# Segmented attention with a memory, mixed with a gated FFN: two weight loads cut in halves, the gate row spread by its transfer, and the order of the work written anew

## The chip, the cores and the metric

The kernel runs on one core of one Trainium2 chip. The metric is the device time of one execution in microseconds. The kernel before takes 268.12 us, the median of 3 runs (267.37 to 268.38).

In this document TensorE is PE (its weight loads are PEld), VectorE is DVE, ScalarE is ACT, GpSimd is POOL, and SyncE is SP, which here only issues transfers (SPq in the profile).

## The reference

The input x has 2048 rows of 512 numbers, in bf16. Three results are formed from it and mixed row by row:

```python
x = A_x
g = _sigmoid((x * gate_w).sum(-1, keepdims=True))
a = _A_ref(x, A_wq, A_wk, A_wv, A_wo, A_beta)
b = _B_ref(x, B_W_gate, B_W_up, B_W_down)
return g * a + (1 - g) * b
```

`_A_ref` is attention with 32 heads of 16 columns, over 4 segments of 512 rows. Inside a segment it is a causal softmax; in addition each head has a memory matrix M and a norm z, both sums over all earlier segments, and `beta` mixes the two by head:

```python
num = jnp.einsum('bhld,bhde->bhle', pq, M)
den = jnp.einsum('bhld,bhd->bhl', pq, z)[..., None] + 1e-06
o = g * (num / den) + (1.0 - g) * a_dot
```

`_B_ref` is a feed-forward part with 1792 hidden columns, `(relu(x @ W_gate) * (x @ W_up)) @ W_down`.

## The kernel before, in words

**Steps and order.** The kernel doesn't issue its instructions directly. Each piece of work is a step: a name, the engine or engines that may do it, the steps it comes after, and a function that emits it (`Plan.add`). A list of numbers, `ORDER` (lines 41 to 100), then fixes for each engine which step comes when: the number v stands for step v // 5 on engine v % 5 of PE, ACT, DVE, POOL, QSP (the queue of SP). `Plan.lay_out` (line 137) walks these five queues and hands out the PSUM banks; it has costs and landing times of its own, which decide nothing but which of the four banks a step gets. Between engines the tile framework adds the waits that the data need.

**PSUM.** Four banks `rb` of 512 columns take all products but the scores; a step that takes a bank waits until an earlier one has been copied out of it. The scores have one tile, `sp`, of four banks; so a score block waits until the exp of the block before it has read `sp`.

**The step names that matter here.** Digits behind a name are the segment and the index.
- XP, XA: transpose of a tile of x on PE (16 small matmuls for segment 0), and its copy to `xT` (ACT or DVE).
- VI and VC: V of segment 0, one 512-column matmul for each tile t and each quarter ci of the depth (VI30 is tile 3, quarter 0); VC copies it out. All four VI of a tile share a bank. V101 and so on are V products of the next segment.
- Q00, K00 and so on: Q or K of a segment, 128 columns each, four matmuls (line 486); QC, KC copy them out; KO is a masked copy of K; EK and EQ are exps of K and Q for the memory, MN, MQ, PK, PQ what follows them; KX transposes PK's result by a transfer.
- G0_0, U0_0 and so on: 128 hidden columns of W_gate or W_up, four matmuls (line 903); R (relu) and H (product) copy them out.
- QK000 to QK008: nine blocks of scores of a segment's first two units, EX000 and so on their exps (line 755, on ACT, the longest step of ACT), MK the causal mask on POOL, PV the product with V.
- GB and GC: described below. TG: the row sums x * gate_w (line 574, DVE, four of them, one per tile of x); TC, TE follow them.
- YP, YD, YA, YH: the gates by heads, from two small loads into `gin`. YP takes a bank and YD (lines 420 and 421, DVE) frees it.
- XT1: the load of x for segment 1 by a transposing transfer, into the place where segment 0's plain x stood, so it comes after the XP and all TG.
- D, DB, W: the product with W_down in two halves, and with wo, of one tile of rows.

**The start.** x and the weights of segment 0 are loaded by `early` (line 345), outside the ordered queues and in the order of the code: on SP x tile 0, wv's first, third and fourth quarter, x tiles 2 and 3, all of wk, two small gate loads into `gin`, all of wq; on ACT x tile 1, wv's second quarter, and `gate_w` as one row of 1 KB. Behind wq the queue of SP goes on with pieces of W_gate and W_up (columns cut at 256, 768 and 1280).

TG needs `gate_w` on all 128 partitions. The row lands in one partition of a zeroed tile, `grow`; GB multiplies it on PE with a matrix of ones, and GC copies the result to `gwb`:

```python
def row_mm(e, s):
    nc.tensor.matmul(rb[s.bank][:], lhsT=ones[:], rhs=grow, start=True, stop=True)
rm = add("GB", {"PE": 0.3}, row_mm, after=[gr_in], prio=-900.0, take=True, lat=0.25)
```

**Around the change.** Before PE begins on K it waits for the whole of wk; before Q for the whole of wq. The first steps of PE are, in order, the warm-up, XP00 to XP11, VI and GB mixed, XP20, XP21, VI02, VI03, XP31, XP30, then:

```
VI20 VI21 VI22 VI23 VI30 VI31 VI32 K00 K01 Q00 VI33 G0_0 YP QK000 K03 K02 Q03 QK001
G0_1 G0_2 Q01 QK002 U0_1 U0_0 V111 QK003 ...
```

The functions that the change touches:

Of the kernel before, what the change touches and what calls it, by code (L numbers as in the profile page):

```python
# [12 lines left out]
P = 128  # L13
# [28 lines left out]
    69, 125, 130, 140, 160, 136, 150, 167, 350, 156, 355, 146, 375, 215, 380, 221, 385, 390, 170, 180, 397, 360, 176,  # L42
    365, 186, 200, 190, 400, 206, 405, 197, 79, 371, 410, 467, 415, 425, 89, 430, 421, 435, 472, 260, 71, 285, 94,
    267, 250, 272, 292, 84, 440, 1070, 257, 104, 446, 462, 225, 505, 976, 335, 477, 511, 99, 983, 310, 232, 342, 214,
    325, 236, 1081, 242, 518, 996, 520, 1090, 317, 526, 1002, 1110, 1007, 987, 1014, 275, 1101, 533, 332, 1016, 535,
    282, 1095, 994, 541, 322, 1075, 454, 1107, 1580, 297, 109, 1036, 1022, 550, 1587, 1450, 556, 1122, 459, 1475,
    1042, 482, 1457, 1510, 486, 1482, 493, 565, 1087, 300, 571, 1027, 1150, 1034, 307, 1600, 1517, 1641, 578, 580,
    1162, 1130, 586, 1607, 1047, 1485, 548, 1647, 1054, 1460, 1656, 1491, 595, 1662, 114, 1155, 1467, 248, 601, 1667,
    1525, 1167, 119, 1500, 1497, 1531, 608, 1142, 2406, 610, 1620, 2386, 1190, 1506, 1627, 563, 616, 2392, 1135, 1115,
    1147, 625, 2412, 1201, 1652, 640, 631, 1127, 1210, 647, 1472, 1055, 1686, 2397, 1221, 740, 497, 2404, 1215, 1062,  # L50
    746, 652, 1068, 657, 667, 1590, 1227, 1270, 672, 1597, 1671, 1275, 677, 1693, 2426, 1281, 755, 2432, 1560, 761,
    638, 1195, 1287, 662, 1250, 1207, 346, 770, 2417, 593, 1330, 1261, 1677, 776, 1697, 1170, 623, 1567, 1255, 682,
    2437, 1181, 785, 1341, 1267, 1535, 2444, 791, 768, 1682, 1610, 1542, 2424, 690, 1617, 1701, 2446, 1723, 800, 783,
    697, 1175, 806, 717, 1750, 1230, 1187, 753, 1757, 722, 1570, 1762, 1241, 1767, 815, 2452, 702, 1780, 1576, 1772,
    1310, 821, 2457, 1550, 707, 1787, 2464, 1792, 1315, 1797, 1321, 828, 830, 1556, 124, 1327, 1840, 1235, 836, 1708,
    1847, 1802, 1290, 1852, 1639, 1857, 1247, 1725, 845, 712, 798, 1732, 1335, 1862, 851, 1302, 1295, 1737, 1742,
    1347, 813, 2465, 2864, 1307, 860, 727, 1810, 2472, 866, 1350, 1817, 843, 1822, 1747, 1827, 732, 875, 1521, 737,
    873, 1832, 1895, 1355, 902, 1839, 1901, 882, 858, 907, 1865, 2925, 1872, 1877, 887, 1882, 1910, 2932, 2875, 1916,
    502, 2900, 912, 1887, 2882, 2950, 687, 2906, 1925, 917, 2956, 925, 892, 897, 1931, 1400, 932, 922, 3821, 1938,
    952, 2975, 1940, 1547, 957, 2865, 1946, 962, 937, 3828, 1405, 2872, 942, 2936, 967, 1953, 947, 1955, 1375, 972,  # L60
    1961, 1908, 1360, 3056, 1968, 1970, 1367, 1410, 1976, 1374, 1380, 1634, 1923, 1894, 3801, 1985, 3807, 1385, 1417,
    1991, 2982, 1425, 3062, 3832, 1998, 2000, 2030, 2006, 1430, 2037, 2057, 2013, 2477, 2015, 2500, 2021, 1435, 2512,
    2520, 1712, 1441, 2062, 2140, 2532, 2525, 2146, 3812, 2915, 2537, 3025, 1392, 2153, 3035, 3067, 3031, 1399, 2155,
    2921, 2580, 1983, 3839, 3042, 2161, 2042, 2067, 2585, 2028, 2592, 1424, 1779, 2645, 2887, 2047, 2597, 3015, 2912,
    1809, 2170, 3022, 2505, 2176, 2072, 3819, 2640, 2517, 2560, 1449, 2651, 2185, 2657, 2985, 2191, 2890, 2992, 2085,
# [949 lines left out]
```

## Time and profile before

| | |
|---|---|
| Time, median of 3 runs | 268.12 us (267.37 to 268.38) |
| Profiled execution: time | 268.13 us |
| Profiled execution: span | 266.4 us |
| PE busy | 261.1 us (98%) |
| DVE busy | 184.5 us (69%) |
| ACT busy | 184.5 us (69%) |
| POOL busy | 140.1 us (53%) |
| Granted PE clock, mean | 1.0 |

The span runs from the first to the last instruction of the trace; the time of the execution holds 1.7 us more around it. Rows of groups and of the timeline read: start in us and length in us (timeline) or busy time and mean length (groups), engine, line of the kernel, operation, output <- input, shape, count, and in brackets the idle time ahead of it with what ended it. Matmuls are pipelined, so a row's length for several of them is longer than the pitch at which they follow each other; the chain of work gives the pitch. Rows of stretches give, for each engine, the busy time and the instructions begun, then the granted clock, the share of the transfer engines and GB/s.

### The profile page before, as it was taken

The numbers are of one execution on the slowest core, as the hardware profiler recorded it, in microseconds if no ns is written. First come the engines' busy times: TensorE is split into PE (matmuls) and PEld (weight loads), VectorE is DVE, ScalarE is ACT, GpSimd is POOL, SyncE is SP. The second block draws the span as 40 slices with busy tenths as digits, with TensorE's granted clock in tenths as the row PEclk, the third lists the DMA queues.
The fourth block names the chain that finished last, engine by engine and source line by source line (L and its number), as shares of the span: only waits on it lengthen the run. The fifth ranks groups of instructions, "written<-read, shape, count | busy, mean of one in ns | idle before, by whom it ended". The sixth has DMA issues, their size and how long they took to land.

```text
span 266.4 us, 7971 instructions
## 1 busy us (share of the span) xinstructions
PE 261.1 (98%) x3338; PEld 120.9 (45%) x3338; DVE 184.5 (69%) x466; ACT 184.5 (69%) x176; POOL 140.1 (53%) x322
## 2 busy tenths in 40 slices
PE   8899999999999999999999999999999999999995
PEld 5344445445344444444443454444544444444453
DVE  2688868989873685865875657778874278788732
ACT  4397999997678677887766698877655377656001
POOL 7053757968567541576728525648039640556410
PEclk9999999999999999999999999999999999999999
DMA  6996291117302014000500200000043000010302
GB/s 182 312 293 166 53 346 23 40 24 145 58 4 62 2 33 107 2 2 2 124 2 0 61 4 2 0 4 2 2 102 84 20 5 20 2 42 2 79 2 79
DMA packets 32736, 16.64 MB, mean 62 GB/s; under 512 B 20027, under 2 KB 32700, under 8 KB 32700
## 3 DMA queue, kind: packets, MB, share of 16 engines
q1 hardware_dynamic: 32410, 15.87, 23.6%
q8 instruction: 26, 0.43, 0.6%
q10 hardware_dynamic: 290, 0.26, 0.3%
q14 instruction: 10, 0.08, 0.1%
HBM read 8.13 MB, written 2.10 MB: 38 GB/s over the span
## 4 chain that ended last, share of the span: by engine, by line
PE 94%; DMA 4%; SPq 0%; DVE 0%; issue 0%
PE rb L903 38%; PE rb L937 18%; PE rb L486 10%; PE sp L744 10%; PE rb L792 7%; PE rb L950 5%; PE rb L528 4%; DMA wq_sb<-in_A_wq_dram 2%; DMA wv_sb<-in_A_wv_dram 1%; PE rb L687 1%; PE rb L861 1%; PE rb L641 1%; PE rb L869 0%; SPq L346 0%; DVE rg L880 0%
## 5 line engine op out<-in xcount | busy, mean ns | idle before, releaser
L755 ACT ACTIVATE E<-sp 128x2048 bf16<-128x2048 f32 x72 | 135.2, 1877 | 44.2 <-PE sp L744 41.1
L765 POOL TENSOR_SCALAR_AFFINE_SELECT E<-E 64x256 bf16<-64x256 bf16 x256 | 111.5, 435 | 92.0 <-ACT E L755 76.0
L903 PE MATMUL rb<-xT,wu_sb 128*128 128x512 bf16 x224 | 56.2, 380 | 0.0
L903 PE MATMUL rb<-xT,wg_sb 128*128 128x512 bf16 x224 | 55.7, 380 | 0.0
L922 DVE TENSOR_TENSOR hT<-rb,rg 128x512 bf16<-128x512 f32 x56 | 37.8, 680 | 17.9 <-PE rb L903 11.2
L937 PE MATMUL rb<-wd_sb,hT 128*128 128x512 bf16 x210 | 49.5, 380 | 0.0
L903 PEld LDWEIGHTS <-wg_sb 128*128 128x128 bf16 x224 | 20.4, 98 | 25.1 <-issue 4.4
L903 PEld LDWEIGHTS <-wu_sb 128*128 128x128 bf16 x224 | 20.1, 98 | 23.8 <-issue 4.3
L937 PEld LDWEIGHTS <-hT 128*128 128x128 bf16 x210 | 19.4, 98 | 24.3 <-issue 3.3
L744 PE MATMUL sp<-QT,KT 16*64 16x320 bf16 (+7 forms) x512 | 30.3, 295 | 0.0
L744 PE MATMUL sp<-QT,KTo 32*64 32x320 bf16 (+7 forms) x512 | 30.3, 295 | 0.0
L810 DVE STREAM_TRANSPOSE tA<-rb 128x512 f32<-128x512 f32 x32 | 21.9, 702 | 10.4 <-PE rb L792 9.8
L915 ACT ACTIVATE rg<-rb 128x512 bf16<-128x512 f32 x36 | 21.1, 596 | 6.4 <-PE rb L903 4.9
L744 PEld LDWEIGHTS <-KT 16*64 16x64 bf16 x512 | 10.5, 102 | 25.6 <-issue 24.9
L961 DVE TENSOR_SCALAR osb<-rb,ngcol 128x512 bf16<-128x512 f32 x11 | 8.2, 749 | 18.6 <-PE rb L950 18.3
L792 PE MATMUL rb<-E,Vs 64*32 64x448 bf16 (+7 forms) x512 | 18.8, 284 | 0.0
L792 PE MATMUL rb<-E,Vp 64*32 64x448 bf16 (+7 forms) x512 | 18.4, 284 | 0.0
L917 DVE TENSOR_SCALAR rg<-rb 128x512 bf16<-128x512 f32 x20 | 13.7, 684 | 4.9 <-PE rb L903 4.8
L486 PE MATMUL rb<-xT,wq_sb 128*128 128x512 bf16 x64 | 16.2, 380 | 0.7 <-DMA wq_sb<-in_A_wq_dram 0.7
L486 PE MATMUL rb<-xT,wk_sb 128*128 128x512 bf16 x64 | 15.7, 380 | 0.2 <-DMA wk_sb<-in_A_wk_dram 0.2
L950 PE MATMUL rb<-wo_sb,oT 128*128 128x512 bf16 x60 | 14.8, 380 | 0.0
L528 PE MATMUL rb<-wv_sb,xT 128*128 128x257 bf16 (+1 forms) x96 | 14.5, 273 | 0.1
(103 smaller groups left out, 284.5 us busy)
## 6 DMA issues: line engine op xcount, KB each, us to landing
out_dram<-osb SPq DMA_DIRECT2D x15, 128.0 KB, 1.9
wd_sb<-in_B_W_down_dram SPq DMA_DIRECT2D x1, 1792.0 KB, 8.4
wg_sb<-in_B_W_gate_dram SPq DMA_DIRECT2D x3, 512.0 KB, 4.3
wu_sb<-in_B_W_up_dram SPq DMA_DIRECT2D x3, 512.0 KB, 7.3
Vs<-Vp SPq DMA_DIRECT2D x8, 144.0 KB, 3.0
wk_sb<-in_A_wk_dram SPq DMA_DIRECT2D x1, 512.0 KB, 5.0
wq_sb<-in_A_wq_dram SPq DMA_DIRECT2D x1, 512.0 KB, 6.4
wo_sb<-in_A_wo_dram SPq DMA_DIRECT2D x1, 512.0 KB, 5.1
```

The costliest lines, as they stand in the source:

```text
L486: nc.tensor.matmul(rb[s.bank][:], lhsT=w[:, ci, c * P:(c + 1) * P], rhs=xT[i][:, ci, :], start=(ci == 0), stop=(ci == NC - 1))
L528: nc.tensor.matmul(rb[s.bank][:, 0:n], lhsT=xT[i][:, ci, t * P:(t + 1) * P], rhs=wv_sb[:, ci, h * D // 2:h * D // 2 + n], start=(ci == 0), ...
L744: nc.tensor.matmul(sp[64 * h:64 * h + 64, j, off:off + m], lhsT=kt[32 * j:hi, c0 + w, 64 * ck:64 * ck + 64], rhs=QT[i][32 * j:hi, c0 + w, ...
L755: nc.scalar.activation(Er[n % NE][:], sp[:], ACT.Exp, scale=SCALE)
L765: nc.gpsimd.affine_select(out=v, in_=v, compare_op=ALU.is_ge, fill=0.0, base=0, pattern=[[0, 4], [1, 64]], channel_multiplier=-1)
L792: nc.tensor.matmul(rb[s.banks[h]][32 * j:32 * j + 32, q0:q0 + m], lhsT=v[64 * h:64 * h + 64, ck // 2, o:o + 32], rhs=Er[(base + f) % NE][6 ...
L810: nc.vector.transpose(tA[k].rearrange("p b w -> p (b w)"), rb[a.banks[r]][:])
L903: nc.tensor.matmul(rb[s.bank][:], lhsT=w[:, ci, fv * P:(fv + 1) * P], rhs=xT[i][:, ci, :], start=(ci == 0), stop=(ci == NC - 1))
L915: nc.scalar.activation(rgb[k][:], rb[a.bank][:], ACT.Relu)
L922: nc.vector.tensor_tensor(hT[:, fv, :], rb[a.bank][:], rgb[k][:], ALU.mult)
L937: nc.tensor.matmul(rb[b][:], lhsT=hT[:, fv, lc:lc + P], rhs=wd_sb[:, fv, :], start=(fv == 0), stop=False)
L950: nc.tensor.matmul(rb[hold.bank][:], lhsT=oT[i][:, ci, lc:lc + P], rhs=wo_sb[:, ci, :], start=False, stop=(ci == NC - 1))
```

## The change

1. wk is loaded in two transfers, by output columns: 0 to 255, then 256 to 511 (rows of 512 bytes instead of 1024). K00 and K01 come after the first alone, K02 and K03 after the second alone.
2. wq is loaded in two transfers, by rows (two quarters of the depth each). Every Q product comes after both.
3. GB, GC, the row tile `grow` and its memset go. `gate_w` is read by one transfer that repeats the row for all 128 partitions, 128 KB, straight into `gwb`, on SP behind wq.
4. The two small gate loads also move behind wq and the gate row. The order of early loads on SP is now: x tile 0, wv's first, third and fourth quarter, x tiles 2 and 3, wk in two, wq in two, the gate row, the two small loads. ACT issues x tile 1 and wv's second quarter as before.
5. `ORDER` is another list. PE's start is now:

```
... XP21 XP20 VI02 VI03 XP30 XP31 VI20 VI21 VI22 VI23 K01 K00 VI30 K03 K02 Q00 VI31
G0_0 YP QK000 G0_1 VI32 G0_2 VI33 QK001 U0_0 Q03 Q01 QK002 U0_1 V101 Q11 QK003
V111 K10 G0_3 QK004 K12 G0_4 Q13 QK005 Q02 K11 U0_4 QK006 ...
```

ACT's: XA00 XA11 XA21 XA20 XA30 VC00 VC02 KC00 EK01 KC03 QC00 KC02 EK00 EX000 R0_2 YA TE0 EX001 EK02 VC03 EX002 KO01 EX003 (before: XA00 XA10 XA01 GC XA20 XA21 XA31 VC00 VC02 VC03 EK00 EX000 YA R0_0 EK01 EX001).

DVE's: XA10 XA01 VC01 XA31 KC01 KO00 TG01 TG03 TG00 TG02 YD R0_0 TC0 R0_1 (before: XA11 VC01 XA30 TG01 TG02 KC00 KO00 KC01 QC00 TG00 TG03 YD).

SP's, behind the early loads: W_gate's and W_up's first pieces, W_gate's second, W_up's third, XT1, KX00, W_gate's third and fourth, W_up's second (before: both first, both second and both third pieces ahead of XT1).

ACT has 184 steps instead of 175, DVE 417 instead of 429, PE 357 instead of 358.

```diff
-    gwb, xg, grow = mtok[:, 0, :], memT[:, 0, :], memT[:, 1, :]
-    nc.vector.memset(grow, 0.0)
+    gwb, xg = mtok[:, 0, :], memT[:, 0, :]
...
-                     (4.0, 4.2, 5.5, 6.0)[ci]) for ci in range(NC)]
-    gr_in = early("ACT", grow[0:1, :], gate_w.rearrange("(o d) -> o d", o=1), 5.0)
-    xin += [early("SP", xn[:, t, :], x[t * P:(t + 1) * P, :], 6.4 + 0.6 * (t - 2)) for t in (2, 3)]
-    ld["K"] = [early("SP", wk_sb[:], rows(A_wk), 8.7)]
-    ld["gw"] = early("SP", gin[0:NC, 0:P], gate_w.rearrange("(c p) -> c p", p=P), 9.5)
-    ld["beta"] = early("SP", gin[0:1, P:P + H], A_beta.rearrange("(o h) -> o h", o=1), 9.5)
-    ld["Q"] = [early("SP", wq_sb[:], rows(A_wq), 10.1)]
-    e_q = add("E_Q", {"QSP": 8.2}, lambda e, s: None, prio=-2000.0, lat=0.0)
+                     (4.0, 4.2, 5.2, 5.65)[ci]) for ci in range(NC)]
+    xin += [early("SP", xn[:, t, :], x[t * P:(t + 1) * P, :], 6.0 + 0.3 * (t - 2)) for t in (2, 3)]
+    ld["K"] = [early("SP", wk_sb[:, :, h:h + 2 * P], rows(A_wk, h, h + 2 * P), land) for h, land in ((0, 7.9), (2 * P, 9.6))]
+    ld["Q"] = [early("SP", wq_sb[:, h:h + 2, :], rows(A_wq)[:, h:h + 2, :], 10.3 + 0.35 * h) for h in (0, 2)]
+    ld["gr"] = early("SP", gwb, gate_w.rearrange("(o d) -> o d", o=1).to_broadcast([P, D]), 11.4)
+    ld["gw"] = early("SP", gin[0:NC, 0:P], gate_w.rearrange("(c p) -> c p", p=P), 11.6)
+    ld["beta"] = early("SP", gin[0:1, P:P + H], A_beta.rearrange("(o h) -> o h", o=1), 11.6)
+    e_q = add("E_Q", {"QSP": 8.5}, lambda e, s: None, prio=-2000.0, lat=0.0)
...
-    def row_mm(e, s):
-        nc.tensor.matmul(rb[s.bank][:], lhsT=ones[:], rhs=grow, start=True, stop=True)
-    rm = add("GB", {"PE": 0.3}, row_mm, after=[gr_in], prio=-900.0, take=True, lat=0.25)
-
-    def row_out(e, s):
-        cp(e, gwb, rb[rm.bank][:])
-    ld["gr"] = add("GC", {"DVE": dve(D), "ACT": act(D)}, row_out, after=[rm], prio=-900.0, give=rm)
...
-                a = add(f"{what}{seg}{c}", {"PE": mm(L, NC)}, pj, after=d["xT"] + ld[what], prio=want, take=True, lat=0.3)
+                a = add(f"{what}{seg}{c}", {"PE": mm(L, NC)}, pj, after=d["xT"] + (ld["Q"] if what == "Q" else [ld["K"][c // 2]]), prio=want, take=True, lat=0.3)
```

The numbers at the end of the `early` lines are landing times for `lay_out`, not waits.

116 rows, old and new, of the table ORDER are left out of this document.

## The prediction

> **What bounds the kernel now.** First the page's busy shares and its chain, then busy time by stretches, then TensorE's waits.
>
> ```profile
> span 266.4 us, 7971 instructions
> PE 261.1 (98%) x3338; PEld 120.9 (45%) x3338; DVE 184.5 (69%) x466; ACT 184.5 (69%) x176; POOL 140.1 (53%) x322
> ...
> PE 94%; DMA 4%; SPq 0%; DVE 0%; issue 0%
> ```
>
> ```profile
> 5.00:10.00 5.00, 4.83 (x28) 2.27 (x28) 2.29 (x6) 2.87 (x7) 1.13 (x2) 1.00 0.88 261
> 10.00:15.00 5.00, 4.34 (x29) 1.81 (x28) 3.81 (x10) 1.91 (x3) 0.88 (x1) 1.00 1.07 355
> ...
> 30.00:60.00 30.00, 30.00 (x460) 14.24 (x459) 24.60 (x61) 28.60 (x33) 21.56 (x51) 1.00 0.36 103
> 60.00:250.00 190.00, 189.93 (x2554) 85.50 (x2560) 133.01 (x335) 134.14 (x115) 102.75 (x240) 1.00 0.15 33
> ```
>
> ```profile
> PE rb L486 <- DMA wq_sb<-in_A_wq_dram: 0.7, 1, 0.7
> PE rb L391 <- DMA xT<-in_A_x_dram: 0.2, 1, 0.2
> PE rb L486 <- DMA wk_sb<-in_A_wk_dram: 0.2, 1, 0.2
> ```
>
> TensorE is the bound: 94% of the chain, and from 30 to 250 us it is idle 0.07 us. What a rearrangement can win is idle time: 0.17 us between 5 and 10 us (K's weight) and 0.66 between 10 and 15 (Q's weight). The granted clock is 1.00 in each row. Only ACT in 30:60 (28.60 of 30) is near to binding beside TensorE.
>
> The profiled execution took 268.13 us, 1.73 more than its span; the median of the runs is 268.12, so the sum below is made against 268.13 and holds for both.
>
> **The start, where the change lies.** The timeline, with the issues of the SP queue, and the times from issue to landing:
>
> ```profile
> 2.65 1.29 SPq L346 DMA_DIRECT2D xT<-in_A_x_dram  x2
> 3.98 0.43 SPq L346 DMA_DIRECT2D wk_sb<-in_A_wk_dram  x1
> 5.22 0.41 SPq L346 DMA_DIRECT2D wq_sb<-in_A_wq_dram  x1
> 5.22 0.38 PE L411 MATMUL rb<-memT,ones 128*128 128x512 bf16 x1
> 5.44 0.82 PE L511 MATMUL rb<-wv_sb,xT 128*128 128x512 bf16 x3
> 5.67 1.41 SPq L325 DMA_DIRECT2D wg_sb<-in_B_W_gate_dram  x2
> 6.09 0.46 PE L391 MATMUL rb<-ident,xT 128*128 128x128 bf16 x4
> 9.06 1.90 PE L486 MATMUL rb<-xT,wk_sb 128*128 128x512 bf16 x8 [0.16 <-DMA wk_sb<-in_A_wk_dram]
> 11.62 1.04 PE L486 MATMUL rb<-xT,wq_sb 128*128 128x512 bf16 x4 [0.66 <-DMA wq_sb<-in_A_wq_dram]
> ```
>
> ```profile
> wk_sb<-in_A_wk_dram SPq DMA_DIRECT2D x1, 512.0 KB, 5.0
> wq_sb<-in_A_wq_dram SPq DMA_DIRECT2D x1, 512.0 KB, 6.4
> xT<-in_A_x_dram SPq DMA_DIRECT2D x3, 128.0 KB, 2.7
> ...
> wg_sb<-in_B_W_gate_dram SPq DMA_DIRECT2D x1, 256.0 KB, 6.7
> wu_sb<-in_B_W_up_dram SPq DMA_DIRECT2D x1, 256.0 KB, 7.8
> ...
> xT<-in_A_x_dram SPq DMA_TRANSPOSE x3, 4.1
> ```
>
> Issue plus landing: the last tile of x about 6.3 (3.6 + 2.7), K 9.0, Q 11.6, the first piece of W_gate 12.4. So 512 KB takes about 2.6 us here, though only 1.2 us lie between two issues: the transfers queue, and bytes ahead set the landing.
>
> The waits of the SP queue itself:
>
> ```profile
> SPq L346 <- DMA xT<-in_A_x_dram: 0.5, 1, 0.5
> ```
>
> This one stands before the last tile of x, the ninth early transfer, until the first has landed. I read it as a limit of eight under way: a transfer's issue also waits for the one eight before it.
>
> Block lengths, from the chain in order of time (four 512-column matmuls 0.86, 0.97 straight after a score block; a 256-column projection 0.44; a score block 0.35):
>
> ```profile
> 13.78 0.35 PE sp L744 x8
> ...
> 16.83 0.36 PE sp L744 x16
> ...
> 22.07 0.44 PE rb L528 x4
> ...
> 25.91 0.97 PE rb L486 x4
> 26.88 0.86 PE rb L903 x4
> ```
>
> **The gate-row matmul goes (GB).** From 5.22 to 5.44: 0.22 us of TensorE. Its copy GC (ACT) and the memset (DVE) lie on engines that wait for TensorE there; without them nothing that ends a wait is earlier. Only some 0.1 to 0.2 shows at once, because the next transposes wait for x.
>
> **K sooner.** Before, TensorE was ready for K at 8.90 (9.06 less the wait). Anew, three V products (VI30 to VI32; 0.86 / 4 = 0.216 each, 0.65) stand behind K and GB is gone: ready at 8.90 - 0.65 - 0.15 = 8.1. Columns 0 to 255 of K's weight must be there. Bounds: 7.65 (half of the 2.7 us that K took behind x) and 9.0 (both halves flow together and end as one did). I take 8.0, near the lower: the second half is issued behind the first, and landings in the rows follow issue order. Then K01, K00 to 9.85, VI30 to 10.05, K03, K02 to 11.8. The second half is wanted at 10.05; K as a whole landed at 9.0, so it has 1 us to spare, which also holds what twice as many runs of 512 bytes cost.
>
> The Trainium skill, "DMA: Bandwidth & Descriptors", section "Why small descriptors are slow (HBM only)", speaks against the split: some 3 cycles of overhead per packet beside one per 32 bytes, so two runs of 512 bytes cost 38 cycles where one of 1024 costs 35. By the rule K's 2.6 us would become 2.8, an estimate, and the sum 0.1 to 0.2 us less good at most, if K's first half is what TensorE waits for; no row of this trace separates it.
>
> **Q.** All of Q's weight is wanted at 11.8 (Q00 waits for both halves; the split by rows gives TensorE nothing). Its issues move ahead of the two small gate loads, from 5.22 to about 4.6 and 5.1, with as many bytes ahead as before. Bounds: 11.0 (0.6 earlier, as its first issue) and 12.0 (11.6 plus two more issues of 0.4, half of them hidden in the queue). I take 11.6, since bytes, not issues, set it before: no wait. So Q00 starts at 11.8 instead of 11.62, but K02 and K03 are done by then (2 x 0.865 = 1.73) and two V products fewer (0.43), and GB's 0.22 no longer exists elsewhere: ahead by 1.73 - 0.43 - 0.18 = 1.12 us. Check: waits of 0.16 and 0.66, GB 0.22, some 0.1 of slack among the first V products.
>
> **What is late next: ACT.**
>
> ```profile
> 12.91 0.59 ACT L374 CAST Vp<-rb 128x512 bf16<-128x512 f32 x1 [4.04 <-PE rb L511]
> 13.40 0.63 ACT L617 ACTIVATE e1k<-KT 128x512 bf16<-128x512 bf16 x1
> 14.21 1.88 ACT L755 ACTIVATE E<-sp 128x2048 bf16<-128x2048 f32 x1 [0.17 <-PE sp L744]
> 15.98 0.22 ACT L425 ACTIVATE eb<-betac 128x32 f32<-128x32 f32 x1
> ```
>
> There is one score tile, so each score block waits for the exp before it. ACT's new order ahead of EX000 is QC00, KC02, EK00: Q00 ends at 12.65, then 0.1 + 0.59 + 0.59 + 0.63 gives 14.55, exp to 16.45, QK001 at 16.55. TensorE has VI31, G0_0, YP, QK000 to 14.2, then G0_1 0.97, VI32 0.22, G0_2 0.86, VI33 0.22: 16.45. Wait 0.1. EX001 follows R0_2, YA, TE0 (0.59 + 0.22 + 0.2): 17.45 to 19.35; TensorE's U0_0, Q03, Q01 last to 19.6: no wait. EX002 stands behind EK02 and VC03 (1.22): 20.6 to 22.45; TensorE, with U0_1, V101, Q11 (0.97 + 0.44 + 0.86) after QK002, is ready at 22.2: wait 0.3. The next interval comes out even: KO01 (some 0.6) and exp to 24.95 on ACT, V111, K10, G0_3 (0.55 + 0.86 + 0.86) to 25.15 on TensorE. New waits: 0.1 + 0.3 = 0.4.
>
> **DVE and the gate row.**
>
> ```profile
> 13.38 0.68 DVE L574 SCALAR_TENSOR_TENSOR memT<-xT,mtok 128x512 bf16<-128x512 bf16 x1
> 14.10 0.69 DVE L574 SCALAR_TENSOR_TENSOR memT<-xT,mtok 128x512 bf16<-128x512 bf16 x1
> 14.79 0.18 DVE L421 TENSOR_SCALAR betac<-rb 128x32 f32<-128x32 f32 x1
> 14.86 3.61 SPq L337 DMA_TRANSPOSE xT<-in_A_x_dram  x1
> 18.85 2.50 SPq L337 DMA_TRANSPOSE pK<-pkT  x2
> ```
>
> The broadcast row (128 KB) replaces a 1 KB row on another queue and lands behind Q. W_gate's first piece, 256 KB right behind Q, landed 0.8 us after it (12.4 against 11.6), so half of it takes 0.4. Bounds: 11.6 (its reads go on beside Q's) and 13.4 (issued behind Q at 5.6, 7.8 to landing like W_up's first piece). I take 12.1, 0.5 behind Q. Behind it on DVE stand four TG at a pitch of 0.72 (to 15.0), YD (0.3, of which L421 is 0.18) and R0_0. G0_2 needs the bank that YD frees, at 14.2 + 0.97 + 0.22 = 15.4, and YD ends at 15.3: no wait, by 0.1.
>
> The W pieces come later, for the gate row is ahead of them and the limit of eight makes W_up's first piece wait for K's first half and W_gate's second for K's second (9.2). By bytes behind Q: W_gate's first piece 11.6 + 1.2 (384 KB at the same pace) = 12.8, wanted by G0_0 at 12.87; its second after 1152 KB, at the 355 GB/s of the row 10:15, 11.6 + 3.3 = 14.9, wanted by G0_2 at 15.4. YP's two small loads land between, wanted at 13.7. Margins of 0.1 to 0.5: I book 0.05, bounds 0 and 0.6.
>
> The transpose load XT1 waits for the TG as before (15.1 against 14.86; wanted by V101 at 20.9, landing about 19.2). W_up's second piece moves behind XT1 (3.61), KX00 (1.25) and two W_gate pieces: issued about 21, landed by 29 at 7.8; U0_4 wants it at 30.4.
>
> **Order elsewhere.** The lists hold the same products; changes between full, row-tiled and column-tiled matmuls are 164 in both, so TensorE's work is equal. Between EX000 and EX028 ACT does 30 steps beside the exps before and 29 after. I book nothing, with 0.4 either way. In the last 7 us, after the last PV, five D or DB blocks (1.5 each) and more cover the chain to the last oT, as now. Out of the sum: 0.
>
> **Sum.** -1.12 + 0.4 + 0.05 = -0.67: 268.13 becomes 267.46, given as 267.4.
>
> **Rivals.**
> (a) The first half of K does not come early, because both halves land together at 9.0. For: 512 KB takes 2.6 us whatever the issue distance. Against: landings in issue order. Price: 9.0 - 8.1 = 0.9 at K01, less the 0.05 booked for W_gate, which then is in time: 268.3, no change.
> (b) Slower: the gate row holds DVE. TG, YD and R0_0 stand in order, so from a landing of 12.2 on each us of delay keeps G0_2, and with it TensorE, a us longer; XT1 follows. At 12.9 the gain is gone; from 14.2 on (12.2 + 0.67 + 1.34) it is slower by over 0.5%. At the bound 13.4: 267.46 + 1.2 = 268.7. For: W pieces issued right after Q took 6.7 to 7.8, and one row in memory is read 128 times, which no row of this trace prices. Against: only 0.5 us of bytes stand between it and Q.
> (c) The new order waits for ACT between 20 and 60 us: a score block, its exp and two copies or exps of 0.6 take 0.35 + 1.88 + 1.2 and two hand-offs of 0.1, 3.6 us, against 3.05 between the first two score blocks, 13.78 and 16.83, in the old order's chain. ACT idles 1.4 us in 30:60; if half of the 18 intervals lose 0.15, that is 1.4: 268.8. Against: one step less on ACT there, and no wait at all in the old order.
> (d) More is won: the waits on exp (0.4) stay hidden and the order elsewhere gives its 0.4: 266.6. The idle time of the start alone (1.12) doesn't reach 0.5%.
>
> **Numbers.** Forecast 0.50, (a) 0.15, (b) 0.13, (c) 0.12, (d) 0.10. A measurement tells about 0.5% (1.34 us) from no change: faster is below 266.78, slower above 269.46. Below 266.78 lies (d) and a little of the forecast: 0.12. Above 269.46 lie the far ends of (b) and (c), each with about half of its chance, since several waits can meet: 0.13. Same: 0.75. Range: 266.5 to 269.2; the forecast's own, with (a) at its end, 266.9 to 268.4.
>
> **What would show it.** Right: no wait on Q's weight, K's first products at 8.0 to 8.2, QK001 at 16.5 to 16.8 with G0_1 and G0_2 ahead of it, TensorE busy 260.9. Wrong: K01 waiting past 8.5; DVE's first TG after 12.9; idle TensorE with DVE or ACT as releaser in 15 to 60 us; a wait on W_gate or W_up.

## The result, and the profile after

| | before | after |
|---|---|---|
| Time, median | 268.17 us (267.37 to 268.86, 13 runs) | 267.18 us (266.76 to 267.51, 13 runs) |
| Profiled execution: time, span | 268.13, 266.4 us | 266.76, 265.0 us |

The ratio is 0.996, with a 95% interval of 0.9947 to 0.9972: 0.99 us less, a small gain, and less than the 0.5% at which the prediction counts a kernel as faster. In the kernel after, the lines of the code stand 9 or 10 lower than before: 486 is 477 (Q and K), 511 is 502 (V), 744 is 735 (scores), 755 is 746 (exp), 903 is 894 (W_gate, W_up), 574 is 565 (TG), 421 is 412 (YD).

The page of the kernel after, then the stretches shown of before (length, then busy time and instructions of PE, PEld, DVE, ACT and POOL, the granted clock, the share of the transfer engines, GB/s):

```profile
span 265.0 us, 7943 instructions
PE 258.1 (97%) x3293; PEld 121.0 (46%) x3337; DVE 181.0 (68%) x449; ACT 189.7 (72%) x185; POOL 143.7 (54%) x328
```

```profile
5.00:10.00 5.00, 4.68 (x26) 2.07 (x26) 1.59 (x3) 2.10 (x5) 1.12 (x2) 1.00 0.99 312
10.00:15.00 5.00, 5.00 (x32) 2.29 (x31) 3.64 (x13) 3.66 (x7) 0.31 (x1) 1.00 0.89 295
```

Between 10 and 15 us TensorE is busy all the time (before: 4.34 of 5). Between 5 and 10 it still idles 0.32, more than before. PE's total is no evidence here: the page has 3293 matmuls beside 3337 weight loads, so some 44 matmul records are missing, and the 258.1 with them. TensorE's waits are the better view (engine, line, releaser: us, times, longest):

```profile
PE rb L380 <- DVE zeros L252: 1.0, 1, 1.0
PE rb L502 <- DMA wv_sb<-in_A_wv_dram: 0.3, 1, 0.3
PE rb L390 <- DMA xT<-in_A_x_dram: 0.3, 1, 0.3
PE rb L928 <- issue: 0.2, 1, 0.2
```

The waits on K's weight (0.2) and on Q's (0.7) are gone, and none on W_gate, on DVE's gate work or on an exp has come in their place. What is left at the start is earlier: wv and x.

The timeline of the kernel after, SP's issues and TensorE's start, and the times from issue to landing of single transfers (K's first and second half, Q's first and second):

```profile
3.64 0.99 SPq L345 DMA_DIRECT2D wk_sb<-in_A_wk_dram  x2
4.67 1.02 SPq L345 DMA_DIRECT2D wq_sb<-in_A_wq_dram  x2
5.73 0.47 SPq L345 DMA_DIRECT2D mtok<-in_gate_w_dram  x1
6.96 0.40 SPq L324 DMA_DIRECT2D wg_sb<-in_B_W_gate_dram  x1
...
14.67 2.20 SPq L336 DMA_TRANSPOSE xT<-in_A_x_dram  x1
5.66 0.74 PE L502 MATMUL rb<-wv_sb,xT 128*128 128x512 bf16 x2 [0.26 <-DMA wv_sb<-in_A_wv_dram]
6.36 0.40 PE L390 MATMUL rb<-ident,xT 128*128 128x128 bf16 x4
8.27 1.89 PE L477 MATMUL rb<-xT,wk_sb 128*128 128x512 bf16 x7
...
11.94 1.03 PE L477 MATMUL rb<-xT,wq_sb 128*128 128x512 bf16 x4
```

```profile
wk_sb<-in_A_wk_dram SPq DMA_DIRECT2D x1, 256.0 KB, 3.7
wk_sb<-in_A_wk_dram SPq DMA_DIRECT2D x1, 256.0 KB, 4.1
wq_sb<-in_A_wq_dram SPq DMA_DIRECT2D x1, 256.0 KB, 4.2
wq_sb<-in_A_wq_dram SPq DMA_DIRECT2D x1, 256.0 KB, 5.1
...
wg_sb<-in_B_W_gate_dram SPq DMA_DIRECT2D x1, 256.0 KB, 5.4
...
mtok<-in_gate_w_dram SPq DMA_DIRECT2D x1, 128.0 KB, 5.9
```

K's first half landed at about 7.3 (3.64 + 3.7), its second at about 8.2; Q whole at 10.3 (5.2 + 5.1); the gate row at 11.6 (5.73 + 5.9); W_gate's first piece at about 12.3 (6.96 + 5.4). TensorE reached K only at 8.27: K's weight was there before it was wanted.

The chain of waits of the kernel after, the score blocks and what lies between the first of them (start us, length us; before, the first, second and fourth score block began at 13.78, 16.83 and 22.51):

```profile
14.08 0.35 PE sp L735 x8
14.43 0.97 PE rb L894 x4
15.40 0.21 PE rb L502
15.62 0.86 PE rb L894 x4
16.48 0.22 PE rb L502
16.70 0.36 PE sp L735 x16
...
22.38 0.35 PE sp L735 x16
```

**Where the time came from.** The first score block begins 0.30 us later than before (14.08 against 13.78), but K02 and K03 are done by then (1.73 us of work), and only two V products are left over (VI32 and VI33, 0.43). The lead is 1.73 - 0.43 - 0.30 = 1.00 us. At the second score block (16.70 against 16.83) after has done G0_1 and G0_2 where before has done Q03, so the lead is 0.86 + 0.13 = 0.99. Carried on over every score block in this way, with the order lists and the block lengths of the chain, the lead stays between 0.98 and 1.01 up to the twelfth block of the third segment, at 157 us. At the thirteenth it rises to 1.22, and at the last block it is 1.27. The rise is at one place: V301, four 257-column matmuls behind a PV. In the chain it takes 0.79 us before (159.09 to 159.88, with 0.07 of issue between) and 0.55 after (the last line):

```profile
159.09 0.22 PE rb L528
...
159.38 0.50 PE rb L528 x3
...
161.00 0.55 PE rb L519 x4
```

The same rise of 0.22 to 0.24 at that block, and of 0.26 to 0.28 by the last block, is in all twelve profiles of kernels with the new order. In the one other profile with the old order V301 takes 1.02 us. So this part belongs to the order, though it lies far behind the start; what holds V301 up in the old order isn't shown.

The profiled execution of the kernel after is the shortest of its 13, 0.42 us below their median. From the first score block's first matmul to the end it takes 251.0 us, and so do the other two profiles of this kernel (last section); the kernel before takes 252.7 (266.4 less 13.71), with 1.30 us more work left (1.73 - 0.43). So about 0.35 of the gain is made behind the first score block. Of the 0.99 of the medians that leaves some 0.6 ahead of it, an estimate, for only one execution of the kernel before was profiled.

### The profile page after: what moved, and what is told of

It reads as the page before. It is cut to its first block, busy times and chain, and to the rows that moved or that the text cites. A ratio compares the mean times of both kernels' runs of the same rounds, so it can differ in the third digit from the quotient of the medians.

```text
span 265.0 us, 7943 instructions
## 1 busy us (share of the span) xinstructions
PE 258.1 (97%) x3293; PEld 121.0 (46%) x3337; DVE 181.0 (68%) x449; ACT 189.7 (72%) x185; POOL 143.7 (54%) x328
## 4 chain that ended last, share of the span: by engine, by line
PE 94%; DMA 1%; DVE 1%; issue 1%; ACT 1%; SPq 0%
PE rb L894 36%; PE rb L928 17%; PE rb L477 11%; PE sp L735 9%; PE rb L783 7%; PE rb L941 5%; PE rb L519 4%; DMA wv_sb<-in_A_wv_dram 1%; PE rb L678 1%; PE rb L852 1%; PE rb L502 1%; DVE hT L913 1%; ACT E L746 1%; PE rb L632 1%; PE rb L860 0%
## 5 line engine op out<-in xcount | busy, mean ns | idle before, releaser
L894 PE MATMUL rb<-xT,wu_sb 128*128 128x512 bf16 x208 | 54.9, 380 | 0.8
L928 PE MATMUL rb<-wd_sb,hT 128*128 128x512 bf16 x198 | 48.6, 380 | 0.8 <-issue 0.2
L801 DVE STREAM_TRANSPOSE tA<-rb 128x512 f32<-128x512 f32 x32 | 21.9, 700 | 12.0 <-PE rb L783 11.6
L735 PEld LDWEIGHTS <-KT 16*64 16x64 bf16 x512 | 10.5, 102 | 27.5 <-issue 26.9
L950 ACT ACTIVATE osb<-rb,ngcol 128x512 bf16<-128x512 f32 x8 | 5.5, 691 | 16.2 <-PE rb L941 16.2
L952 DVE TENSOR_SCALAR osb<-rb,ngcol 128x512 bf16<-128x512 f32 x7 | 5.2, 750 | 16.1 <-PE rb L941 15.9
L812 DVE TENSOR_TENSOR o<-tA,co 128x256 bf16<-128x256 f32 x32 | 15.4, 493 | 0.2
```

Source lines behind the costliest of these rows:

```text
L735: nc.tensor.matmul(sp[64 * h:64 * h + 64, j, off:off + m], lhsT=kt[32 * j:hi, c0 + w, 64 * ck:64 * ck + 64], rhs=QT[i][32 * j:hi, c0 + w, ...
L801: nc.vector.transpose(tA[k].rearrange("p b w -> p (b w)"), rb[a.banks[r]][:])
L812: nc.vector.tensor_tensor(o16[u % 2][:, :, r, :], tA[k][:, :, 0:DH], cos[k][:, :, None].to_broadcast([P, NB, DH]), ALU.mult)
L894: nc.tensor.matmul(rb[s.bank][:], lhsT=w[:, ci, fv * P:(fv + 1) * P], rhs=xT[i][:, ci, :], start=(ci == 0), stop=(ci == NC - 1))
L928: nc.tensor.matmul(rb[b][:], lhsT=hT[:, fv, lc:lc + P], rhs=wd_sb[:, fv, :], start=(fv == 0), stop=False)
```

## The experiments

The question was which part made the 1.0 us: the cut of K, the cut of Q, the row without its matmul, the place of the small loads, or the order. And why it is 1.0 and not the 0.7 that was forecast. The kernels below stood in three groups, each run beside the kernel before, with medians of 268.14, 268.08 and 268.16 for it.

### The changed kernel again, as the measure of each group

No edit; once in the first group, once in the third.

> The changed kernel once more, beside the variants: 1.0 us faster than before (0.996), with K's two halves landed at about 7.3 and 8.2 us, Q's second half at 10.3, and the gate row at 11.6.

> The changed kernel beside the next three: 267.0 to 267.2 us.

Measured: 267.03 us (266.81 to 267.53; ratio 0.9956, 0.9939 to 0.9972) and 266.84 us (266.55 to 267.68; 0.9955, 0.994 to 0.9971). The gain is 1.1 and 1.3 us here, within the interval of the first measurement; the second median is a little below the 267.0 expected. All 25 runs of the changed kernel lie between 266.55 and 267.68.

### The loads without the order

The changed kernel's loads, with the order of before, less GB and GC; the first two TG stand behind QC00, since the gate row comes late.

```diff
+ (loads, gate row and the waits of Q and K as in the changed kernel)
- ORDER of the changed kernel
+ ORDER of the kernel before, without GB and GC; DVE: ... QC00 TG01 TG02 TG00 TG03 YD ...
```

> The loads of the changed kernel with the order of the kernel before (GB and GC left out, the first two TG moved behind QC00 on DVE, since the gate row lands later now). If the order is what turns the sooner loads into time, then Q00 starts at about 10.5 without a wait, but G0_0 stands at 11.6 and waits for W_gate's first piece until 12.4: the lead over the kernel before is 0.2 to 0.4 us (267.8 to 268.0). If the loads alone are the gain, the lead is 1.0 us as in the changed kernel (267.2).

Measured: 268.9 us (267.9 to 269.59), ratio 1.0018 (1.0004 to 1.0033): slower than before, and neither of the times expected. TensorE's waits in this kernel, then its timeline and DVE's:

```profile
PE rb L477 <- DVE betac L412: 0.8, 1, 0.8
...
PE rb L390 <- DMA xT<-in_A_x_dram: 0.6, 1, 0.6
```

```profile
11.62 1.03 PE L477 MATMUL rb<-xT,wq_sb 128*128 128x512 bf16 x4
...
16.76 1.02 PE L477 MATMUL rb<-xT,wq_sb 128*128 128x512 bf16 x4 [0.81 <-DVE betac L412]
15.83 0.69 DVE L565 SCALAR_TENSOR_TENSOR memT<-xT,mtok 128x512 bf16<-128x512 bf16 x1
...
16.52 0.18 DVE L412 TENSOR_SCALAR betac<-rb 128x32 f32<-128x32 f32 x1
```

The waits on K and Q are gone here too, and W_gate is not waited for. Yet Q00 begins at 11.62 as before, and not at the 10.5 expected: TensorE came to K only at 9.89, after a wait of 0.6 for the first tile of x and six slow V products (last section). Then YD stands behind four TG on DVE; the last TG begins at 15.83 and YD at 16.52, and Q03 waits 0.81 us for the bank that YD frees. This is rival (b)'s mechanism. The new order has QC00 and KC00 on ACT, and Q03 behind G0_2; so DVE copies fewer things ahead of the TG. What follows: as arranged here the loads alone win nothing, and with the late gate row the old order is worse than before. The cut loads in the old order with the gate row by matmul were not run, so the share of the late row in this loss isn't shown.

### The order without the cuts

The changed kernel with K and Q each in one transfer, and the small gate loads back between them, as before. The gate row stays a repeated row of 128 KB behind Q.

```diff
-    ld["K"] = [early("SP", wk_sb[:, :, h:h + 2 * P], rows(A_wk, h, h + 2 * P), land) for h, land in ((0, 7.9), (2 * P, 9.6))]
-    ld["Q"] = [early("SP", wq_sb[:, h:h + 2, :], rows(A_wq)[:, h:h + 2, :], 10.3 + 0.35 * h) for h in (0, 2)]
-    ld["gr"] = early("SP", gwb, ...)
+    ld["K"] = [early("SP", wk_sb[:], rows(A_wk), 8.0)] * 2
     ld["gw"] = ...
     ld["beta"] = ...
+    ld["Q"] = [early("SP", wq_sb[:], rows(A_wq), 11.0)]
+    ld["gr"] = early("SP", gwb, ...)
```

> The changed kernel's order and broadcast gate row, but K and Q in one transfer each and the two small loads between them, as in the kernel before. If the order (K02 and K03 ahead of Q) and the missing GB make the gain, and the cuts only help landings, it is 267.2 to 267.8, with K landed by 8.4. If the cuts make it, K lands near 9.0 and the gain over the kernel before is at most 0.3: 267.8 to 268.1.

Measured: 267.46 us (267.07 to 267.63), ratio 0.9972 (0.996 to 0.9983). TensorE's timeline, and K's landing:

```profile
8.71 1.90 PE L477 MATMUL rb<-xT,wk_sb 128*128 128x512 bf16 x7 [0.24 <-DMA wk_sb<-in_A_wk_dram]
```

```profile
wk_sb<-in_A_wk_dram SPq DMA_DIRECT2D x1, 512.0 KB, 5.1
```

0.7 us of gain (268.16 to 267.46) is there without any cut, of 1.3 in this group and 1.0 in the first measurement: half to seven tenths. The order and the missing gate-row matmul make that part. In this profile (267.29 us) the lead is 0.54 at the first score block, where four K products ahead of Q give Q's weight the time to land, and 0.82 at the last block. K landed at 8.7, and not by the 8.4 expected.

### K whole, Q in halves

```diff
-    ld["K"] = [early("SP", wk_sb[:, :, h:h + 2 * P], rows(A_wk, h, h + 2 * P), land) for h, land in ((0, 7.9), (2 * P, 9.6))]
+    ld["K"] = [early("SP", wk_sb[:], rows(A_wk), 8.0)] * 2
```

> The changed kernel with K's weight in one transfer again, all else the same. If the split is what lets TensorE begin on K sooner, K lands as a whole near 9.0 as in the kernel before, K01 waits some 0.7 us, and 0.7 of the 1.0 us is lost (267.9). If the loads as a whole land sooner because nothing small stands between them and their issue is earlier, K lands near 8.3, TensorE is ready then anyway, and at most 0.2 us is lost (267.2 to 267.4).

Measured: 267.78 us (266.92 to 268.58, 12 runs), ratio 0.9985 (0.9971 to 0.9999): 0.75 more than the changed kernel beside it. But its profiled execution was its fastest, 266.92, and shows no wait on K at all:

```profile
wk_sb<-in_A_wk_dram SPq DMA_DIRECT2D x1, 512.0 KB, 4.6
```

Issued at 3.60, K whole landed at 8.2, and K01 began at 8.34, beside 8.27 in the changed kernel. The same kernel was profiled once more, for a longer execution.

> K's weight in one transfer once more, for another profile. Its first profiled execution (266.92 us) showed K landed at 8.2 and no wait, while the median of its runs is 267.8. If the loss lies in K's landing, which differs between executions, this execution's time exceeds 266.9 by as much as its K01 waits for the weight. If it shows a longer time with K01 at 8.4 all the same, the loss is elsewhere.

Measured: 268.43 us. TensorE's timeline, then a piece of the chain:

```profile
8.45 1.89 PE L477 MATMUL rb<-xT,wk_sb 128*128 128x512 bf16 x7
...
14.31 1.04 PE L894 MATMUL rb<-xT,wg_sb 128*128 128x512 bf16 x4 [0.96 <-DMA wg_sb<-in_B_W_gate_dram]
```

```profile
16.88 0.10 DVE betac L412
...
17.02 1.02 PE rb L894 x4
```

Again no wait on K. Most of the time was lost on W_gate's first piece, which landed at 14.3 and made G0_0 wait 0.96 us. Some 0.25 more went at G0_2, which began at 17.02, when YD had freed its bank: the gate row had landed at 13.5, and this is rival (b)'s mechanism in the new order. W_gate's wait gave a new theory: K in one transfer delays what is behind it, and G0_0 pays.

### G0_0 later, with K in halves and whole

If W_gate's landing is the cause, a kernel that wants it later must lose the cost of K whole. In TensorE's order Q03 takes the place of G0_0, and G0_0, G0_1, G0_2 stand one place later; DVE and ACT are ordered to match (DVE: YD QC03 TC0 R0_0 ... PK01 R0_2; ACT: R0_1 in the place of R0_2).

```diff
- ... Q00 VI31 G0_0 YP QK000 G0_1 VI32 G0_2 VI33 QK001 U0_0 Q03 Q01 QK002 ...
+ ... Q00 VI31 Q03 YP QK000 G0_0 VI32 G0_1 VI33 QK001 G0_2 U0_0 Q01 QK002 ...
```

> The changed kernel with Q03 put where G0_0 stood, and G0_0, G0_1, G0_2 one place later each (their copies too): the first use of W_gate's first piece moves from 13.0 to 14.4 us. If that piece's landing, which was seen from 12.0 to 14.3, is what now makes executions differ, the median falls by 0.1 to 0.3 to 266.9 and the highest run stays below 267.4. If the spread comes from elsewhere, no change; if the copies' new places on ACT and DVE make score blocks wait, it is slower by 0.2 to 0.5.

> The same order with K's weight in one transfer. If what K in one transfer cost (0.7 us in the median) was W_gate's late landing, as its second profile shows, the cost is gone with this order: within 0.2 us of the run before it. If K itself lands late in some executions, 0.5 us or more is left.

Measured: with K in halves 267.16 us (266.95 to 267.47), ratio 0.9961 (0.9948 to 0.9973); with K whole 267.77 us (267.04 to 268.56), ratio 0.998 (0.997 to 0.9991). Still 0.6 apart. In the profile of the second (267.65 us) W_gate landed at 13.5, wanted at 14.97, and K at 8.74, with TensorE ready at 8.87; neither was waited for. (TensorE came to K that late because its first six V products took 2.58 us, beside 1.80 in the second profile of the changed kernel; see the last section.) So the theory falls: W_gate's landing explains the one profile in which it was late, and not the cost of K whole. The later G0_0 also gains nothing on the changed kernel: 267.16 beside 266.84. It has a price of its own, as its expectation allowed: a V product behind the fourth score block waits 0.2 us for a copy of Q on DVE, and the lead in its profile falls there from 0.79 to 0.57.

K whole against K in halves, in one group each: medians 0.75, 0.62 and 0.62 higher (the last with Q whole and the small loads moved too), means 0.67, 0.53 and 0.41 higher, with 0.35, 0.30 and 0.42 as twice their standard errors. The cut of K thus seems to be worth about half a us. In four profiles of kernels with K whole, K01 began at 8.34, 8.45, 8.71 and 8.87, and waited for K in one of them, for 0.24. How K whole loses the rest isn't shown by any profile here, and stays open: TensorE was ready for K at 8.34 to 8.87 in these four, and at 8.07 to 8.48 in the six with K in halves that leave the work ahead of K and wv's loads alone, too few to tell.

### Q whole, K in halves

```diff
-    ld["Q"] = [early("SP", wq_sb[:, h:h + 2, :], rows(A_wq)[:, h:h + 2, :], 10.3 + 0.35 * h) for h in (0, 2)]
+    ld["Q"] = [early("SP", wq_sb[:], rows(A_wq), 11.0)]
```

> The changed kernel with Q's weight in one transfer. Q landed at 10.3 in two parts and is wanted at 11.9 to 12.1, all of it at once. So no change: 267.0, within 0.2. If splitting as such makes landings sooner or steadier, as it may for K, Q lands past 12 in some executions and the median goes up by 0.2 or more.

Measured: 267.06 us (266.9 to 268.01), ratio 0.9967 (0.9956 to 0.9978): as the changed kernel. The cut of Q is worth nothing, as the prediction had it. Its profiled execution was its longest, 268.01, and the waits tell most of it:

```profile
PE rb L894 <- DMA wg_sb<-in_B_W_gate_dram: 0.6, 1, 0.6
```

Another 0.3 went at G0_2, which waited for YD, as in the second profile of K whole; the gate row had landed at 13.1.

### The small loads between K and Q

```diff
     ld["gw"] = ...
     ld["beta"] = ...
+    ld["Q"] = ...
+    ld["gr"] = ...
```

> The changed kernel with the two small gate loads between K's and Q's weight again. If bytes ahead set the landings, Q comes 0.6 us later at most (10.9), still ahead of the 11.9 at which TensorE wants it: no change in time. If the small loads themselves held the queue in the kernel before, Q lands near 11.6 and the gate row near 12.9, DVE begins on TG later by 1.2 us, G0_2 waits for the bank that YD frees, and 0.4 to 0.8 us is lost.

Measured: 267.26 us (266.81 to 268.01), ratio 0.9964 (0.995 to 0.9978), 0.2 more than the changed kernel beside it and inside both intervals. Their place is worth nothing that can be measured.

### The gate row by the matmul again

The row of 1 KB on ACT's queue, `grow`, GB (behind VI10) and GC (ACT, behind XA11) come back; all else is as in the changed kernel.

```diff
+    gr_in = early("ACT", grow[0:1, :], gate_w.rearrange("(o d) -> o d", o=1), 5.0)
-    ld["gr"] = early("SP", gwb, gate_w.rearrange("(o d) -> o d", o=1).to_broadcast([P, D]), 11.4)
+    rm = add("GB", {"PE": 0.3}, row_mm, after=[gr_in], prio=-900.0, take=True, lat=0.25)
+    ld["gr"] = add("GC", {"DVE": dve(D), "ACT": act(D)}, row_out, after=[rm], prio=-900.0, give=rm)
```

> The changed kernel with the gate row by matmul again: a row of 1 KB on ACT's queue, GB behind VI10 on PE, GC behind XA11 on ACT, no broadcast transfer. If GB costs only its own time, 0.2 us is lost (267.2 to 267.3). If the row's place among the eight transfers under way counts too, K's weight is issued 0.35 us later, K01 waits 0.2 to 0.4, and 267.5 to 267.7 comes out. If the late landing of the broadcast row cost something in the changed kernel, this is no slower (267.0).

Measured: 267.36 us (266.7 to 268.1), ratio 0.9968 (0.9951 to 0.9985). TensorE's timeline in its profile (267.03 us):

```profile
5.17 0.38 PE L410 MATMUL rb<-memT,ones 128*128 128x512 bf16 x1
...
7.42 0.40 PE L391 MATMUL rb<-ident,xT 128*128 128x128 bf16 x4 [0.49 <-DMA xT<-in_A_x_dram]
```

That is 0.17 to 0.33 more than the changed kernel and its near relatives (267.19, 267.06, and 267.03 in the first group), each difference about as large as its uncertainty. GB's 0.22 stands here ahead of a wait for x of 0.49, so the profile doesn't part the two. The row on ACT's queue is one more transfer under way: the last tile of x is issued at 3.56 instead of 3.12 and lands at 7.4 instead of 6.7, and that is the wait of 0.49. K's issue moves from 3.64 to 3.93, but K isn't waited for. So the row by matmul may cost more than GB's own time.

### A quarter of wv on ACT's queue

The next wait is wv's third quarter and a tile of x, which share SP's queue; so wv's fourth quarter was moved.

```diff
-    ld["V"] = [early(("SP", "ACT", "SP", "SP")[ci], wv_sb[:, ci, 0:D], A_wv[ci * P:(ci + 1) * P, :],
+    ld["V"] = [early(("SP", "ACT", "SP", "ACT")[ci], wv_sb[:, ci, 0:D], A_wv[ci * P:(ci + 1) * P, :],
```

> The changed kernel with wv's fourth quarter issued by ACT instead of SP, so that x's tiles 2 and 3, K and Q are issued 0.45 us sooner. If issues bound the first 6 us, TensorE's waits on wv and x shrink by 0.2 to 0.4: 266.7. If bytes bound them, nothing changes: 267.0. If ACT's table load, now 0.45 us later, delays its first copy of x, it is slower by 0.1 to 0.3.

Measured: 267.19 us (267.0 to 267.37), ratio 0.9964 (0.9951 to 0.9978): no gain. In its profile no wait on wv is listed, but four of the first six V products are slow (last section), and x is waited for, for 0.6 us instead of 0.3. This is x's first tile, issued at 0.79 in every profile and landed at 3.3 to 3.8; the edit can't have moved it. So the profile doesn't tell why nothing was gained. No kernel tried here beats the changed one.

## Why the prediction was right, point by point

- **Sum.** 267.4 forecast, 267.18 measured: -0.67 by the sum, -0.99 by the medians. The mechanism was right (the idle time ahead of K and Q goes, by order, and no later wait gives it back). That the number fits so well is partly luck, for several terms were off. Between the two profiled executions, 1.37 us apart, the lead at the start is -1.00 (forecast -1.12), the waits on exp 0 (+0.4), W_gate 0 (+0.05) and the order elsewhere about -0.35 (0). In an execution as long as the median the lead at the start is only some 0.6; there the start gave half a us less than its term, and the exps and the order elsewhere 0.75 more.
- **The lead at the start, -1.12: measured -1.00.** Q00 began at 11.94 and not 11.8, without a wait on Q, as predicted. TensorE was ready for K at 8.27 and not at 8.1, for wv's third quarter came 0.26 late and the transposes of x began at 6.36 instead of 6.09. So the sign "K's first products at 8.0 to 8.2" was missed by a little. The term assumed that the work ahead of K runs as before. It doesn't even from one execution to the next: K01 began at 8.07, 8.27 and 8.44 in the three profiles of this kernel, and the lead was 1.20, 1.00 and 0.83.
- **K.** The first half was put at 8.0 (bounds 7.65 and 9.0) and landed at 7.3; in nine profiles of kernels with K in halves it landed between 7.1 and 8.3, the second half between 8.2 and 9.4. Rival (a), both halves together at 9.0, came in none. But K whole, too, landed at 8.1 to 8.7 in the four profiles that have it, and not at 9.0, with an issue at 3.6 instead of 3.98. So the step "the first half lets K01 begin at 8.1" gives the cut a part that the landings don't show: TensorE was ready at 8.27 and could have begun on K whole then or at most 0.4 later. The runs give the cut half a us all the same, by a way that no profile shows.
- **The cost of the cut.** The sentence of the Trainium skill that was weighed ("DMA: Bandwidth & Descriptors", section "Why small descriptors are slow (HBM only)") would put the whole of K 0.2 later, an estimate. The rows lean that way, with the second half at a median of 8.9 and K whole at 8.1 to 8.7; but the second half is also issued half a us later, and nothing here separates the two. The first half, which TensorE wants first, was waited for in none of the nine profiles.
- **Q.** Put at 11.6 (bounds 11.0 and 12.0), landed at 10.3, outside the bounds on the good side. "Bytes, not issues, set it" was wrong for this distance: with its two halves issued 0.55 earlier and at the same time as before (4.67 and 5.2 against 5.22) it landed 1.3 earlier here, and 0.1 to 2.1 earlier in the other profiles; for the old landing there is one profile. The step's conclusion (no wait) holds with more room. That TensorE gains nothing by Q's cut is shown by Q whole: 267.06.
- **The new waits on exp, +0.4: measured 0.** This term was mis-sized. Rows of ACT in the kernel after:

```profile
13.00 0.58 ACT L373 CAST QT<-rb 128x512 bf16<-128x512 f32 x1 [1.14 <-PE rb L477]
13.48 0.59 ACT L373 CAST KT<-rb 128x512 bf16<-128x512 f32 x1
13.96 0.64 ACT L608 ACTIVATE e1k<-KT 128x512 bf16<-128x512 bf16 x1
14.51 1.88 ACT L746 ACTIVATE E<-sp 128x2048 bf16<-128x2048 f32 x1
...
19.51 0.59 ACT L373 CAST Vp<-rb 128x512 bf16<-128x512 f32 x1
20.18 1.88 ACT L746 ACTIVATE E<-sp 128x2048 bf16<-128x2048 f32 x1
21.95 0.71 ACT L490 ACTIVATE KTo<-KT,mcol_o 128x512 bf16<-128x512 bf16 x1
```

  The sum added row lengths: 0.59 + 0.59 + 0.63 = 1.81 for QC00, KC02 and EK00. They begin 0.48, 0.48 and 0.55 apart, 1.51 in all, and the next step begins 1.77 after an exp of 1.88: rows on ACT overlap by about 0.1. The quoted rows of before already showed it, 12.91 to 13.40 being 0.49 for a row of 0.59. The third exp (EX002) began at 20.18 and ended at 22.06, where 22.45 was predicted; TensorE was ready for QK003 at 22.38, where 22.2 was predicted. At QK001 the exp's end was right (16.39, predicted 16.45), since the copies began 0.25 later than assumed; there it is TensorE that came later, 16.70 instead of 16.45: 0.14 with Q00, and some 0.1 by which the sum had placed the end of QK000 too early. The Trainium skill has the overlap ("ScalarE: Activation LUTs", section "What ACT_TABLE_LOAD costs": back-to-back ACTIVATEs overlap by about 93 ns); the trace agrees, with 0.09 and 0.11 behind an ACTIVATE, and shows 0.10 and 0.11 behind a CAST too, which the page doesn't name.
- **The gate row and DVE.** Put at 12.1 (bounds 11.6 and 13.4), landed at 11.6, the lower bound, by two errors that cancel: Q came 1.3 sooner than predicted, and the row 1.3 behind Q, where the step had 0.5. TG began at 11.70 and YD ended at 14.78:

```profile
11.70 0.69 DVE L565 SCALAR_TENSOR_TENSOR memT<-xT,mtok 128x512 bf16<-128x512 bf16 x1 [0.54 <-DMA wu_sb<-in_B_W_up_dram]
...
14.60 0.18 DVE L412 TENSOR_SCALAR betac<-rb 128x32 f32<-128x32 f32 x1
```

  (The releaser named, W_up, isn't read by this step; the gate row landed at 11.6.) G0_2 wanted the bank at 15.6, so there were 0.8 us to spare, and XT1 was issued at 14.67, where 15.1 was predicted. Rival (b) did not come here. It came in the old order with the same loads (0.81 us), and in the new order, for 0.25 to 0.3, in the two profiles whose gate row landed past 13 (13.1 and 13.5). Its argument for, that one row read 128 times has no price, was well put: see the last section.
- **W_gate, +0.05: 0 in the profile shown.** First piece at 12.3 (predicted 12.8), wanted at 13.0. The upper bound of 0.6 was justified: with the same order it was late by 0.64 and 0.96 in two other profiles, those of Q whole and K whole. The limit of eight transfers under way, read from one wait, holds in the kernel after: SP waits 0.3 us for K's weight ahead of W_gate's second piece (issued at 8.21, K's second half landed at 8.2) and 0.3 for Q's ahead of W_up's third (8.89, Q's first half landed at 8.9), each the transfer eight before.
- **GB, 0.22.** 0.17 to 0.33 by the runs with the matmul put back, each about as large as its uncertainty.
- **Order elsewhere, 0 booked with 0.4 either way.** About -0.35: nothing up to 157 us (the lead stays at 0.98 to 1.01), 0.23 at V301, 0.05 in the last segment and 0.1 in the last 20 us; the last 0.1 may be chance, since the old order with the new loads has half of it too. The step "what a rearrangement can win is idle time" missed V301's 0.24: only 0.07 of it, all of the 0.07 that the prediction counts from 30 to 250 us, is idle time, and the rest stands in the rows as busy. Rival (c) did not come; TensorE has no wait on ACT behind 15 us.
- **Rival (d)** had the waits on exp hidden and 0.4 more from the order elsewhere, for 266.6. Both came, nearly; what is missing in the median is at the start, some 0.5 of the 1.12. The shortest execution of the changed kernel, with a lead of 1.20 at the start, took 266.55.

## What to carry to other kernels

Where an engine waits for two loads in turn, look first for work that the first load already allows and put it ahead of the second: four K products ahead of Q, with one small matmul less and the rest of the new order, gave 0.7 us without any cut, about half of it at the start. Follow the gain in a fixed order of work by what is done at the same mark (here the score blocks), since the mark itself came 0.3 us later while the kernel was 1.0 us ahead. Take the pitch at which steps follow each other, and not the length of their rows, when adding up an engine's time. Before a profile's lead is taken for the gain, see where its execution stands among the runs: here it was the shortest.

## What the runs showed of the hardware that was not expected

- **The repeated row is dear for the transfers.** The table below has the landings (issue plus time to landing) of profiled executions, in us. W_gate's first piece, 256 KB, landed 0.7 to 0.8 behind Q where no row stands between them (before, and with the row by matmul), and 1.5 to 3.3 behind Q in the twelve profiles that have the row of 128 KB between them. The row alone landed 0.3 to 2.5 behind Q, 1.6 in the median; 128 KB at the 295 GB/s of the stretch would be 0.4, worked out. So the row seems to be what brought W_gate near to being late, and late in two profiles, though only two profiles are without it. A kernel with the row behind W_gate's first piece was not tried.
- **Executions of the same kernel differ at the start, and by more than landings.** With the same order of TensorE behind K01, nearly all of the difference between executions is there by the first score block, and the rest takes 251 us. Where W_gate was in time, that block begins 5.74 to 5.76 behind K01 (8.07 to 8.87), whether Q landed at 9.5 or 10.6 and the gate row at 11.2 or 12.5. K01 in turn begins 2.2 to 2.3 behind the sixth V product, but for two profiles with a later wait. The six come late when they wait for wv's quarters (0.26 in the kernel after), or when the first of them are slow. But for such waits their pitch is 0.22 us in the kernel after; in other profiles up to five of the first six follow each other at 0.40 to 0.43, and all six in the old order with the new loads. The granted clock of these stretches reads 1.00 all the same; what ends the slow pitch isn't shown. The six in the second profile of the changed kernel (one slow) and in that of the later G0_0 with K whole (five slow):

```profile
4.37 1.80 PE L502 MATMUL rb<-wv_sb,xT 128*128 128x512 bf16 x6
4.46 2.58 PE L502 MATMUL rb<-wv_sb,xT 128*128 128x512 bf16 x6
```

  The table shows eight profiles; in the last two G0_0 waited for W_gate:

| profiled execution | K | Q | gate row | W_gate | K01 begins | first score block | span | from there to the end |
|---|---|---|---|---|---|---|---|---|
| changed kernel, c_after2 | 7.1, 8.7 | 10.6 | 12.0 | 12.7 | 8.07 | 13.81 | 264.8 | 251.0 |
| changed kernel, after | 7.3, 8.2 | 10.3 | 11.6 | 12.3 | 8.27 | 14.01 | 265.0 | 251.0 |
| changed kernel, c_after | 7.5, 9.2 | 10.5 | 11.3 | 12.0 | 8.44 | 14.18 | 265.2 | 251.0 |
| row by matmul, e5_row_matmul | 8.3, 9.1 | 10.5 | - | 11.2 | 8.53 | 14.27 | 265.3 | 251.0 |
| K whole, e1_k_whole | 8.2 | 9.5 | 11.2 | 12.0 | 8.34 | 14.08 | 265.2 | 251.1 |
| wv's quarter on ACT, e6_wv_act | 7.6, 8.3 | 9.9 | 12.5 | 13.2 | 8.87 | 14.61 | 265.7 | 251.0 |
| Q whole, e7_q_whole | 8.3, 9.4 | 11.2 | 13.1 | 13.9 | 8.36 | 14.92 | 266.3 | 251.4 |
| K whole, e1b_k_whole | 8.1 | 11.4 | 13.5 | 14.3 | 8.45 | 15.32 | 266.7 | 251.4 |

  (The start of the score block is that of its first matmul in the timeline; the chain puts it 0.07 later.) One profile tells little of a load that is nearly late.
